# Two-layer mixture of experts behind a channel attention: the gate step of a block of the first layer moves from the steps of the block before it to the block's own

## The chip, the cores and the metric

The kernel runs on one core of a Trainium2 chip. The metric is the time of one execution in microseconds (us) on the device. Engines are named as in the profile: PE is TensorE (PEld its weight loads), DVE is VectorE, ACT is ScalarE, POOL is GpSimd, SP is SyncE. L1891 is line 1891 of the kernel.

## The reference

Three stages run one after the other on 2 x 5056 tokens of 256 channels. The attention's output is the input of the first layer of experts, whose output is the input of the second.

```
# attention over channels (q, k normalised down the tokens)
s = kn.transpose(0, 2, 1) @ qn / tau
a = exp(s - s.max(-1));  a /= a.sum(-1) + 1e-9
x = v @ a                                    # 10112 x 256

# first layer: each token goes to its best of 8 experts
logits = x @ w_gate
e_idx = argmax(logits, axis=1)
gate_w = softmax(logits)[n, e_idx]
eom = 1 / (1 + exp(-(x @ w_output_gate)))
out[mask] = gate_w * eom[:, e] * (relu(x[mask] @ w1[e]) @ w2[e])    # F = 1024

# second layer: experts with a capacity of N // 8, filled in order of the logits
```

The output weight of a first-layer token, gate_w * eom, is one number g for each token. The second layer's gate logits are a product of the first layer's output, so its assignment can only be made when the whole first layer is done.

## The kernel before, in words

The attention is computed first, and each token's row is written to a table in memory (xe_scr). A row holds the 256 channels, the token's gate logits relative to its best one and its output-gate logit (from column ZC on), and a few more numbers (from TC-1 on: the token's number and the like). Rows of one expert are then brought together by indirect transfers.

The first layer works in 33 blocks. A block holds nt = 4, 2 or 1 tiles of 128 tokens, all of one expert. The blocks are taken in the order 4, 4, 1, 2, 4, 2, 4, 1, 2, 4, 4, 1, 2, ... A product in full precision is made of three at lower precision: every operand is split into a high part, which ACT copies, and a low part, which DVE gets by a subtraction (w1h and w1l, w2h and w2l, xh and xl in xhl, hh and hl). One-tile blocks take their first product undivided.

One loop goes over the units of the blocks: 8 of a four-tile block, 4 of the others. In each turn three things are written down, and the framework's scheduler then orders them on each engine, by the buffers that they need and by when it thinks they can run; each engine runs its own queue strictly in that order:

- *ffn1* of the unit: the matmuls pb (L1942), then ACT's hh (L1951) and DVE's hl (L1952).
- *drain* of the unit two turns earlier: the matmuls py (L1970, or L1976 for blocks whose second product is put off until after the second layer's assignment has begun; those need only the gating product py <- hl, gs). Behind a block's last unit stand its output (yout or lout: yo, and l, the second layer's logits, L2004) and order, which makes the key and code rows of the second layer's assignment out of l.
- some *steps* that prepare later blocks, a few per turn from a list that is made at a block's first unit. It has the split steps of block j+1 (s1: w1, L1903 and L1904; sx: transposes of xi, L1882, and xhl, L1884 to L1887; s2: w2, L1908 and L1909; s3: the second layer's gate weights, L1919) and the slot steps of block j+4 (reach: sof and shs, L1672 and L1674; pick: the matmul pt <- tb, shs, L1680; left and count: srl and sju; index: ssi, L1694, which is the list of the rows to fetch). At the same place the weights of block j+2 are loaded (SP, L1814 to L1825), and the rows xi of block j+3 fetched by indirect transfers on POOL, one for each tile (L1697).

The gate step sg is one of the split steps. It takes the logits out of xi into z (L1891, cut at -87), copies the other columns to xk (L1892), and makes g1: an exponential by a polynomial on DVE (the rows gte_t, gte_k, gte_i, L1001 to L1014, with z changed in place), a sum, an add, a product and a reciprocal (L1899). It is 19 DVE rows. yout and lout read xk and g1. z (name z1) has two buffers, xk and g1 three each.

Ahead of the loop stand the split steps of block 0, the fetch of block 1, and the slot steps and fetches of blocks 2 and 3. What stands before that, up to some 208 us, is the end of the attention; the row base (L1558) is one of the last rows of the first layer's assignment.

Of the kernel before, what the change touches and what calls it, by code (L numbers as in the profile page):

```python
# [8 lines left out]
F32 = mybir.dt.float32  # L9
# [13 lines left out]
P = 128  # L23
# [16 lines left out]
AT4, AT1 = (1, 8, 12, 15), (1, 5, 7, 10)  # L40
# [865 lines left out]
def moe_kernel(ctx, tc, q, k, v, tau, wg, wo, w1, w2, wg2, w12, w22, out):  # L906
# [87 lines left out]
    def exp_poly(*args):  # L994
        for _ in exp_steps(*args):
            pass
# [869 lines left out]
    def split_steps(j):  # L1866
# [8 lines left out]
        g1 = pg1.tile([P, nt], F32, name="g1", bufs=3)  # L1875
        xk = pg1.tile([P, nt, XW - TC + 1], F32, name="xk", bufs=3)
        wts[j] = (xk, w1h, w1l, w2h, w2l, xhl, None, g1)
# [10 lines left out]

        def sg(_):
            z = pg1.tile([P, nt, E + 1], F32, name="z1")  # L1890
            V.tensor_scalar(z, xi[:, :, ZC:ZC + E + 1], -87.0, None, op0=ALU.max)  # L1891
            V.tensor_copy(xk, xi[:, :, TC - 1:])  # L1892
            ee = pg1.tile([P, nt, E + 1], F32, name="ee1")
            exp_poly(pg1, ee, z, [P, nt, E + 1], "gte")
            s8 = pg1.tile([P, nt], F32, name="s81")
            V.tensor_reduce(s8, ee[:, :, :E], axis=AX.X, op=ALU.add)
            V.tensor_scalar(s8, s8, 1e-9, None, op0=ALU.add)
            V.scalar_tensor_tensor(s8, ee[:, :, E], 1.0, s8, op0=ALU.add, op1=ALU.mult)
            V.reciprocal(g1, s8)  # L1899
# [21 lines left out]
        steps = [(s1, 0), (sx, 0), (s1, 1), (s1, 2), (sx, 1), (s1, 3), (s2, 0), (s2, 1), (s2, 2), (s2, 3), (sg, 0), (s3, 0)]  # L1921
        return steps if nt > 1 else [x for x in steps if x[0] is not s1]

# [92 lines left out]
    for f_, a_ in [x for i in (0, 2, 3, 5, 1, 4, 6, 7, 8, 9, 10) for x in st_[i:i + 1]] + st_[11:]:  # L2016
        f_(a_)
    ma.close()
    fetch(1)
    for f_, a_ in slot_steps(2):  # L2020
        f_(a_)
    fetch(2)
    for f_, a_ in slot_steps(3):
        f_(a_)
# [21 lines left out]
    for (j, u, n) in units:  # L2046
        if u == 0:
# [3 lines left out]
            if j + 3 < NBLK:  # L2051
                fetch(j + 3)
            if j + 2 < NBLK:
                load(j + 2)
            if j + 4 < NBLK:
                for i, x in zip(AT1 if len(steps) < 12 else AT4, slot_steps(j + 4)):
                    steps.insert(i, x)
            if j in put_off:
                hold(j)
# [3 lines left out]
        for _ in range(SPL[blk(j)[0]]):  # L2063
            if steps:
                f_, a_ = steps.pop(0)
                f_(a_)
    while pend:
        drain()
# [142 lines left out]
```

## Time and profile before

| what | value |
|---|---|
| median of 3 runs | 1385.28 us (1382.11 to 1388.48) |
| the profiled execution, its own time | 1379.16 us |
| its span | 1377.1 us |
| busy, share of the span: PE, PEld | 93%, 84% |
| busy, share of the span: DVE, ACT, POOL | 78%, 58%, 19% |
| granted clock of PE, mean | 0.97 |
| chain that ended last, by engine | PE 43%, DVE 5%, DMA 3%, ACT 1% |

The time is that of the whole execution as the device measures it; the span is from the first to the last instruction that the profiler recorded, so some 2 us lie around it. An engine's busy share counts only its computing instructions. The granted clock is the share of full speed at which TensorE was allowed to run. The chain goes back from the last instruction, at each step to what released it.

### The profile page before, as it was taken

The numbers are of one execution on the slowest core, as the hardware profiler recorded it, in microseconds if no ns is written. First come the engines' busy times: TensorE is split into PE (matmuls) and PEld (weight loads), VectorE is DVE, ScalarE is ACT, GpSimd is POOL, SyncE is SP. The second block draws the span as 40 slices with busy tenths as digits, with TensorE's granted clock in tenths as the row PEclk, the third lists the DMA queues.
The fourth block names the chain that finished last, engine by engine and source line by source line (L and its number), as shares of the span: only waits on it lengthen the run. The fifth ranks groups of instructions, "written<-read, shape, count | busy, mean of one in ns | idle before, by whom it ended". The sixth has DMA issues, their size and how long they took to land.

```text
span 1377.1 us, 25616 instructions
## 1 busy us (share of the span) xinstructions
PE 1281.4 (93%) x8716; PEld 1154.5 (84%) x8716; DVE 1069.5 (78%) x3756; ACT 798.5 (58%) x1752; POOL 267.3 (19%) x367
## 2 busy tenths in 40 slices
PE   8999998999799988999899896989999999999997
PEld 6899866898688977878887896879999999998996
DVE  6887678699588967797688677998999898987321
ACT  5566665466365554574467565766667585755222
POOL 1000012112012021020020002141325051416312
PEclk9999998999899999999999998999999999999999
DMA  8869758196657577095572695030303030314100
GB/s 283 283 218 341 235 164 259 37 296 203 214 163 279 178 249 226 30 340 171 157 242 74 216 409 176 24 116 23 112 29 121 28 119 33 107 63 156 43 24 30
DMA packets 138915, 222.88 MB, mean 162 GB/s; under 512 B 26432, under 2 KB 102336, under 8 KB 136736
## 3 DMA queue, kind: packets, MB, share of 16 engines
q1 hardware_dynamic: 112496, 174.29, 37.5%
q0 software_dynamic: 11808, 32.69, 8.1%
q10 hardware_dynamic: 14480, 14.27, 3.3%
q8 instruction: 69, 1.13, 0.3%
q14 instruction: 62, 0.51, 0.1%
HBM read 170.18 MB, written 50.31 MB: 160 GB/s over the span
## 4 chain that ended last, share of the span: by engine, by line
PE 43%; DVE 5%; DMA 3%; ACT 1%; issue 1%; POOL 1%; DVEq 0%; POOLq 0%; ACTq 0%
PE pb L777 15%; PE py L818 15%; PE pd L2155 4%; PE pb L1942 3%; PE py L1970 2%; DVE junk L377 1%; DMA xi<-xe_scr,ssi 1%; PE pb L739 1%; PE py L816 1%; DMA xi<-y_scr,si 1%; ACT junk L380 1%; PE pb L1937 1%; DVE hl L798 0%; DMA w1r<-in_moe_w_dram 0%; POOL xi L686 0%
## 5 line engine op out<-in xcount | busy, mean ns | idle before, releaser
L1942 PE MATMUL pb<-xhl,w1h 128*128 128x512 f32 (+1 forms) x800 | 217.0, 360 | 2.2 <-ACT xhl L1886 1.6
L1697 POOL DMA_INDIRECT xi<-xe_scr,ssi x86 | 87.3, 1016 | 623.9 <-DVE srl L1685 196.2
L1951 ACT ACTIVATE hh<-pb 128x512 fp32r<-128x512 f32 (+1 forms) x180 | 101.5, 565 | 144.9 <-PE pb L1942 121.5
L818 PE MATMUL py<-w2l,hh 128*128 128x256 f32 (+1 forms) x640 | 182.4, 285 | 0.0
L818 PE MATMUL py<-w2h,hl 128*128 128x256 f32 (+1 forms) x640 | 181.7, 284 | 0.0
L818 PE MATMUL py<-w2h,hh 128*128 128x256 f32 (+1 forms) x600 | 173.2, 289 | 0.0
L790 ACT ACTIVATE hh<-pb 128x512 fp32r<-128x512 f32 (+1 forms) x160 | 93.9, 589 | 132.9 <-PE pb L777 127.0
L798 DVE SCALAR_TENSOR_TENSOR hl<-pb,hh 128x512 fp32r<-128x512 f32 (+1 forms) x160 | 108.4, 678 | 69.2 <-ACT hh L790 69.1
L1942 PEld LDWEIGHTS pb<-xhl,w1h 128*128 128x128 f32 x800 | 137.5, 196 | 19.8 <-ACT xhl L1886 1.8
L1970 PE MATMUL py<-w2h,hh 128*128 128x264 f32 x496 | 147.5, 298 | 6.1 <-DVE l L2004 6.0
L1970 PE MATMUL py<-w2h,hl 128*128 128x264 f32 x496 | 144.7, 292 | 5.1 <-DVE hl L1952 5.1
L1970 PE MATMUL py<-w2l,hh 128*128 128x264 f32 x496 | 145.4, 293 | 0.3 <-DVE w2l L1919 0.3
L1942 PE MATMUL pb<-xhl,w1l 128*128 128x512 f32 (+1 forms) x400 | 140.7, 352 | 0.0
L777 PE MATMUL pb<-xl,w1h 128*128 128x256 f32 (+2 forms) x384 | 139.8, 364 | 0.4 <-DVE xl L747 0.4
L777 PE MATMUL pb<-xh,w1h 128*128 128x256 f32 (+2 forms) x384 | 139.4, 363 | 0.2 <-DVE hl L798 0.2
L777 PE MATMUL pb<-xh,w1l 128*128 128x256 f32 (+2 forms) x384 | 138.9, 362 | 0.0
L844 POOL DMA_INDIRECT out_dram<-yo,ti x80 | 79.4, 993 | 282.0 <-ACT yo L836 242.7
L1952 DVE SCALAR_TENSOR_TENSOR hl<-pb,hh 128x512 fp32r<-128x512 f32 (+1 forms) x180 | 114.4, 637 | 24.1 <-ACT hh L1951 23.2
L818 PEld LDWEIGHTS py<-w2l,hh 128*128 128x128 f32 (+1 forms) x640 | 120.5, 188 | 4.2
L818 PEld LDWEIGHTS py<-w2h,hl 128*128 128x128 f32 (+1 forms) x640 | 120.6, 188 | 1.6
L818 PEld LDWEIGHTS py<-w2h,hh 128*128 128x128 f32 (+1 forms) x600 | 113.0, 188 | 3.8
L1970 PEld LDWEIGHTS py<-w2h,hh 128*128 128x128 f32 x496 | 97.0, 196 | 10.6 <-DVE l L2004 7.4
(530 smaller groups left out, 3444.8 us busy)
## 6 DMA issues: line engine op xcount, KB each, us to landing
w2r<-in_moe_w_dram SPq DMA_DIRECT2D x45, 1024.0 KB, 8.3
w1r<-in_moe_w_dram SPq DMA_DIRECT2D x41, 1024.0 KB, 5.5
vt<-in_v_dram SPq DMA_DIRECT2D x18, 512.0 KB, 7.1
qt<-in_q_dram SPq DMA_DIRECT2D x17, 512.0 KB, 3.7
kt<-in_k_dram SPq DMA_DIRECT2D x17, 512.0 KB, 4.5
xe_scr<-xs ACTq DMA_DIRECT2D x8, 1072.0 KB, 5.8
h_scr<-hh SPq DMA_DIRECT2D x32, 256.0 KB, 3.2
h_scr<-hl SPq DMA_DIRECT2D x32, 256.0 KB, 3.6
```

Of the source, the lines that this page charges most:

```text
L377: V.tensor_scalar(junks[c], x, s.cand[:, c:c + 1], 0.0, op0=ALU.is_ge, op1=ALU.add, accum_out=cnt[:, c:c + 1])
L777: T.matmul(x.pb[:, ci, :n], a[:, c, fc * P:fc * P + P], b_[:, c, xs_], start=(c == 0 and i == 0), stop=(c == 1 and i == 2))
L790: S.activation(x.hh[:, :, :n], x.pb[:, :, :n], AF.Relu)
L798: V.scalar_tensor_tensor(x.hl[f], x.pb[f], 0.0, x.hh[f].bitcast(F32), op0=ALU.max, op1=ALU.subtract)
L818: T.matmul(py[:m_, t % 2, :], a[:, ci, t * P:t * P + m_], b_[:, fc, :], start=False, stop=(fc == 7 and i == 2 and t % 2 == 1))
L844: s_ = G.indirect_dma_start(out=out, out_offset=bass.IndirectOffsetOnAxis(ap=st.ti[:m_, t0 + t:t0 + t + 1], axis=0), in_=q.yo[:m_, t % 2, ...
L1697: nc.gpsimd.indirect_dma_start(out=xi[:, i, :], out_offset=None, in_=xe, in_offset=bass.IndirectOffsetOnAxis(ap=self.si[:, i:i + 1], axis=0))
L1942: T.matmul(o, a[:, c, ws], xhl[:, c, h, :], start=(i == 0), stop=(i == 5))
L1951: S.activation(hh, pb, AF.Relu)
L1952: V.scalar_tensor_tensor(hl, pb, 0.0, hh.bitcast(F32), op0=ALU.max, op1=ALU.subtract)
L1970: T.matmul(py[t][:, :width], a[:, ci, ts_], b_[:, fc, :width], start=(fc == 0 and i == 0), stop=(fc == 7 and i == 2))
L2155: T.matmul(py[t][:, :D], a[:, ts_], b_[:, fc, :D], start=(fc == 0 and i == 0), stop=(fc == 7 and i == 2))
```

## The change

The gate step is no longer one of the split steps of the block ahead. It is a function gate_step(j) and stands among the steps that are worked off during block j itself, at place 6 of the list. z and xk become two parts of one buffer, zk, of which there is one: the next block's zk can only be written when yout or lout of the last block has read it. g1 has two buffers in place of three. The slot steps and fetches of blocks 2 and 3 move from the stretch ahead of the loop into the list of block 0, together with those of block 4 (at places 2, 9 and 15; block 0 takes four steps per unit). The places of the slot steps in the other lists shift by one, since the list is one shorter ahead of them. All lists must now be done by their block's last unit.

```
--- before.py
+++ after.py
@@ -37,7 +37,8 @@
 NCH = {4: 1, 2: 2, 1: 2}
 HS, XS, FS = 1, 1, 3
 PLAG, PHB = 2, 4
-AT4, AT1 = (1, 8, 12, 15), (1, 5, 7, 10)
+AT4, AT1 = (1, 8, 11, 14), (1, 5, 7, 9)
+GAT = {4: 6, 2: 6, 1: 6}
 KS1, KS2 = 16, 28
 KST = (KS1, KS2)
 KO4, KO2, KO1 = 0.0, 0.97, 0.5
@@ -1872,9 +1873,7 @@
         w2l = pws.tile([P, 8, D + E], F32R, name="w2l")
         xhl = pxi.tile([P, 2, 2, nt * P], F32R, name="xhl")
         xh, xl = xhl[:, :, 0, :], xhl[:, :, 1, :]
-        g1 = pg1.tile([P, nt], F32, name="g1", bufs=3)
-        xk = pg1.tile([P, nt, XW - TC + 1], F32, name="xk", bufs=3)
-        wts[j] = (xk, w1h, w1l, w2h, w2l, xhl, None, g1)
+        wts[j] = [xi, w1h, w1l, w2h, w2l, xhl, None, None]
 
         def sx(c):
             pt = qt_.tile([P, 512], F32, name="pt")
@@ -1886,18 +1885,6 @@
             S.copy(xh[:, c, :], pt[:, :nt * P])
             V.tensor_tensor(xl[:, c, :], pt[:, :nt * P], xh[:, c, :].bitcast(F32), op=ALU.subtract)
 
-        def sg(_):
-            z = pg1.tile([P, nt, E + 1], F32, name="z1")
-            V.tensor_scalar(z, xi[:, :, ZC:ZC + E + 1], -87.0, None, op0=ALU.max)
-            V.tensor_copy(xk, xi[:, :, TC - 1:])
-            ee = pg1.tile([P, nt, E + 1], F32, name="ee1")
-            exp_poly(pg1, ee, z, [P, nt, E + 1], "gte")
-            s8 = pg1.tile([P, nt], F32, name="s81")
-            V.tensor_reduce(s8, ee[:, :, :E], axis=AX.X, op=ALU.add)
-            V.tensor_scalar(s8, s8, 1e-9, None, op0=ALU.add)
-            V.scalar_tensor_tensor(s8, ee[:, :, E], 1.0, s8, op0=ALU.add, op1=ALU.mult)
-            V.reciprocal(g1, s8)
-
         def s1(i):
             c, f = i // 2, slice(i % 2 * 512, i % 2 * 512 + 512)
             S.copy(w1h[:, c, f], w1r[:, c, f])
@@ -1918,8 +1905,25 @@
                 S.copy(w2h[:, :, D:], wgr)
                 V.tensor_tensor(w2l[:, :, D:], wgr, w2h[:, :, D:].bitcast(F32), op=ALU.subtract)
 
-        steps = [(s1, 0), (sx, 0), (s1, 1), (s1, 2), (sx, 1), (s1, 3), (s2, 0), (s2, 1), (s2, 2), (s2, 3), (sg, 0), (s3, 0)]
+        steps = [(s1, 0), (sx, 0), (s1, 1), (s1, 2), (sx, 1), (s1, 3), (s2, 0), (s2, 1), (s2, 2), (s2, 3), (s3, 0)]
         return steps if nt > 1 else [x for x in steps if x[0] is not s1]
+
+    def gate_step(j):
+
+        nt, xi = blk(j)[0], wts[j][0]
+        zk = pg1.tile([P, nt, E + 1 + XW - TC + 1], F32, name="zk", bufs=1)
+        g1 = pg1.tile([P, nt], F32, name="g1")
+        wts[j][0], wts[j][7] = zk[:, :, E + 1:], g1
+        z = zk[:, :, :E + 1]
+        V.tensor_scalar(z, xi[:, :, ZC:ZC + E + 1], -87.0, None, op0=ALU.max)
+        V.tensor_copy(zk[:, :, E + 1:], xi[:, :, TC - 1:])
+        ee = pg1.tile([P, nt, E + 1], F32, name="ee1")
+        exp_poly(pg1, ee, z, [P, nt, E + 1], "gte")
+        s8 = pg1.tile([P, nt], F32, name="s81")
+        V.tensor_reduce(s8, ee[:, :, :E], axis=AX.X, op=ALU.add)
+        V.tensor_scalar(s8, s8, 1e-9, None, op0=ALU.add)
+        V.scalar_tensor_tensor(s8, ee[:, :, E], 1.0, s8, op0=ALU.add, op1=ALU.mult)
+        V.reciprocal(g1, s8)
 
     def ffn1(j, u, w, nt):
 
@@ -2013,15 +2017,10 @@
     for j in (4, 5):
         sls[j].table()
     st_ = split_steps(0)
-    for f_, a_ in [x for i in (0, 2, 3, 5, 1, 4, 6, 7, 8, 9, 10) for x in st_[i:i + 1]] + st_[11:]:
+    for f_, a_ in [x for i in (0, 2, 3, 5, 1, 4, 6, 7, 8, 9) for x in st_[i:i + 1]] + st_[10:]:
         f_(a_)
     ma.close()
     fetch(1)
-    for f_, a_ in slot_steps(2):
-        f_(a_)
-    fetch(2)
-    for f_, a_ in slot_steps(3):
-        f_(a_)
     units = []
     for j in range(NBLK):
         nt = blk(j)[0]
@@ -2048,22 +2047,29 @@
             steps = split_steps(j + 1) if j + 1 < NBLK else []
             if j + 6 < NBLK:
                 sls[j + 6].table()
-            if j + 3 < NBLK:
+            if 0 < j and j + 3 < NBLK:
                 fetch(j + 3)
             if j + 2 < NBLK:
                 load(j + 2)
-            if j + 4 < NBLK:
-                for i, x in zip(AT1 if len(steps) < 12 else AT4, slot_steps(j + 4)):
+            if not j:
+                for k, i in ((2, 2), (3, 9), (4, 15)):
+                    for x in slot_steps(k) + ([(lambda _, k=k: fetch(k), 0)] if k < 4 else []):
+                        steps.insert(i, x)
+                        i += 1
+            elif j + 4 < NBLK:
+                for i, x in zip(AT1 if len(steps) < 11 else AT4, slot_steps(j + 4)):
                     steps.insert(i, x)
+            steps.insert(GAT[blk(j)[0]], (lambda _, j=j: gate_step(j), 0))
             if j in put_off:
                 hold(j)
         pend.append((j, u, n, ffn1(j, u, wts[j], blk(j)[0])))
         if len(pend) > PLAG:
             drain()
-        for _ in range(SPL[blk(j)[0]]):
+        for _ in range(SPL[blk(j)[0]] if j else 4):
             if steps:
                 f_, a_ = steps.pop(0)
                 f_(a_)
+        assert u < n - 1 or not steps
     while pend:
         drain()
     mp.close()
```

What it does to the order of the instructions, on DVE. The lines of the changed kernel are shifted: z is L1918, xk L1919, hl L1956, l L2008, w2l L1896, w1l L1891, the gate rows L1002 to L1015. A number behind a name tells tiles of the same name apart; x2 means twice in a row.

The first place is the end of block 8 (two tiles) and the two four-tile blocks behind it, 9 and 10. Before, z_5264 belongs to block 9 and z_5565 to block 10, and yo to block 8; the ssi at the top is the list of rows for a later fetch:

```order
L1694 SCALAR_TENSOR_TENSOR ssi<-ssl,pt 128x4
L1952 SCALAR_TENSOR_TENSOR hl<-pb,hh 128x512
L1909 TENSOR_TENSOR w2l<-w2r,w2h 128x2x256 x2
L1952 SCALAR_TENSOR_TENSOR hl<-pb,hh 128x512
L1909 TENSOR_TENSOR w2l<-w2r,w2h 128x2x256
L1892 COPY xk<-xi 128x8
L1899 RECIPROCAL g_4879<-s_5051 128x2
L1919 TENSOR_TENSOR w2l<-wgr,w2h 128x8x8
L1891 TENSOR_SCALAR z_5264<-xi 128x36
L1952 SCALAR_TENSOR_TENSOR hl<-pb,hh 128x512
L1001 TENSOR_SCALAR gte_t<-z_5264 128x36
L2001 COPY yo<-xk 128x2x4
```

The row behind these is the next z:

```order
L1891 TENSOR_SCALAR z_5565<-xi 128x36
L1003 TENSOR_SCALAR gte_k<-gte_t 128x36
L1001 TENSOR_SCALAR gte_t<-z_5565 128x36
L1004 SCALAR_TENSOR_TENSOR z_5264<-gte_k,z_5264 128x36
L1013 TENSOR_SCALAR gte_i<-gte_k 128x36
```

After, at the l rows of block 8 (l_2781 <- py, g_5148) and behind them; the zk row is that of block 9:

```order
L2008 TENSOR_SCALAR l_2781<-py,g_5148,zk 128x8
L1891 TENSOR_TENSOR w1l<-w1r,w1h 128x512
L2008 TENSOR_SCALAR l_2781<-py,g_5148,zk 128x8
L1886 TENSOR_TENSOR xhl<-pt,xhl 128x512
L1791 TENSOR_SCALAR key_t<-l_2781 128x16
L1802 TENSOR_TENSOR ord_g<-l_2781 128x128
L1792 TENSOR_TENSOR key_t<-l_2781,key_t 128x16
L1956 SCALAR_TENSOR_TENSOR hl<-pb,hh 128x512
L1795 COPY key<-key_t 128x8x2 x2
L1803 TENSOR_TENSOR ord_g<-ord_g,tri_226 128x128
L1918 TENSOR_SCALAR zk<-xi 128x4x9
L1919 COPY zk<-xi 128x4x4
```

Before, the z of both blocks stands ahead of the l rows of block 8, with one hl, one gte_t and yo between them. After, zk of block 9 stands behind the l rows of block 8; that of block 10 follows 53 rows later, behind the l rows of block 9.

The second place is a two-tile block, 12, from the key row of the block before it (11, one tile) on. Before:

```order
L1794 COPY key<-key_t 128x8 x2
L1802 TENSOR_TENSOR ord_g<-ord_g,tri_226 128x64
L1904 TENSOR_TENSOR w1l<-w1r,w1h 128x512
L1805 TENSOR_REDUCE ord_a<-ord_g 128x8
L1806 TENSOR_REDUCE ord_b<-ord_g 128x8
L1909 TENSOR_TENSOR w2l<-w2r,w2h 128x2x256
L1807 TENSOR_TENSOR ord_a<-ord_a,ord_b 128x8
L1952 SCALAR_TENSOR_TENSOR hl<-pb,hh 128x512
L1808 SCALAR_TENSOR_TENSOR code<-ord_a,c_228 128x8
L1909 TENSOR_TENSOR w2l<-w2r,w2h 128x2x256 x3
L1952 SCALAR_TENSOR_TENSOR hl<-pb,hh 128x512
L1685 SCALAR_TENSOR_TENSOR srl<-rh,k2o,pt 128x1
```

After:

```order
L1795 COPY key<-key_t 128x8 x2
L1803 TENSOR_TENSOR ord_g<-ord_g,tri_226 128x64
L1918 TENSOR_SCALAR zk<-xi 128x2x9
L1919 COPY zk<-xi 128x2x4
L1806 TENSOR_REDUCE ord_a<-ord_g 128x8
L1807 TENSOR_REDUCE ord_b<-ord_g 128x8
L1002 TENSOR_SCALAR gte_t<-zk 128x18
L1891 TENSOR_TENSOR w1l<-w1r,w1h 128x512
L1808 TENSOR_TENSOR ord_a<-ord_a,ord_b 128x8
L1004 TENSOR_SCALAR gte_k<-gte_t 128x18
L1956 SCALAR_TENSOR_TENSOR hl<-pb,hh 128x512
L1809 SCALAR_TENSOR_TENSOR code<-ord_a,c_228 128x8
```

Before, there is no gate row in this block (they stand in a four-tile block ahead of it); after, the block's own gate rows stand between its w2l, hl and w1l rows and the key and code rows of the block before.

The third place is the start of the experts' part. Before, around the row base_333 of the first layer's assignment:

```order
L1558 TENSOR_TENSOR ones__332<-left,k1n 128x8
L1558 SCALAR_TENSOR_TENSOR ones__332<-ones__332,odd 128x8
L1558 SCALAR_TENSOR_TENSOR base_333<-k1n,base 128x8
L1558 TENSOR_TENSOR tmp_279<-lt,ones__332 128x64
L1558 TENSOR_REDUCE kc_298<-tmp_279 128x8
L1558 TENSOR_SCALAR kc_298<-kc_298 128x8
L1468 TENSOR_TENSOR wl<-pt,wh 128x512
```

After:

```order
L1559 TENSOR_TENSOR ones__332<-left,k1n 128x8
L1559 SCALAR_TENSOR_TENSOR ones__332<-ones__332,odd 128x8
L1559 SCALAR_TENSOR_TENSOR base_333<-k1n,base 128x8
L1918 TENSOR_SCALAR zk<-xi 128x4x9
L1559 TENSOR_TENSOR tmp_279<-lt,ones__332 128x64
L1919 COPY zk<-xi 128x4x4
L1002 TENSOR_SCALAR gte_t<-zk 128x36
L1559 TENSOR_REDUCE kc_298<-tmp_279 128x8
L1004 TENSOR_SCALAR gte_k<-gte_t 128x36
```

After, the zk of block 0 is moved up to right behind base_333, and the following gate rows stand between the rows of the assignment and wl, the last split weights of the attention. The queues of SP and POOL have the same order before and after.

## Rows read from the trace of the kernel before

**Rows 1.** Busy time by stretches: length, busy time per engine, granted clock, DMA share, GB/s.
```profile
210.50:762.50 552.00, 504.77 (x3306) 447.56 (x3306) 437.43 (x1699) 306.43 (x750) 80.75 (x82) 0.95 0.60 194
340.00:380.00 40.00, 30.07 (x188) 27.08 (x187) 24.39 (x105) 14.57 (x33) 5.12 (x5) 0.83 0.69 227
497.00:530.00 33.00, 23.32 (x158) 21.95 (x157) 20.12 (x92) 12.38 (x28) 0.94 (x1) 0.84 0.61 189
645.00:715.00 70.00, 61.49 (x469) 58.76 (x468) 51.71 (x209) 38.72 (x102) 12.52 (x12) 0.96 0.59 190
```

**Rows 2.** VectorE's waits, 210 to 765: total, times, longest.
```profile
DVE z L1891 <- DMA xi<-xe_scr,ssi: 59.4, 16, 7.3
...
DVE z L1891 <- issue: 2.7, 1, 2.7
```

**Rows 3.** TensorE's waits, 210 to 765.
```profile
PE py L1976 <- DVE hl L1952: 13.0, 6, 4.7
...
PE pt L1680 <- DVE xhl L1887: 11.1, 3, 5.3
...
PE py L1970 <- DVE l L2004: 6.0, 3, 2.6
...
PE py L1970 <- DVE hl L1952: 5.1, 1, 5.1
...
PE pt L1882 <- issue: 2.4, 1, 2.4
...
PE py L1975 <- DVE l L2004: 2.0, 1, 2.0
...
PE pt L1680 <- DVE shs L1674: 1.6, 1, 1.6
```

**Rows 4.** Timeline of one stall: start, duration, engine, operation, idle before.
```profile
344.45 0.95 POOL L1697 DMA_INDIRECT xi<-xe_scr,ssi  x1 [0.30 <-issue]
...
350.50 0.18 DVE L1891 TENSOR_SCALAR z<-xi 128x36 f32<-128x36 f32 x1 [6.34 <-DMA xi<-xe_scr,ssi]
...
352.31 0.60 PE L1976 MATMUL py<-hl,gs 128*8 128x512 f32 x1 [4.67 <-DVE hl L1952]
```

**Rows 5.** Timeline of TensorE at two later gaps.
```profile
615.04 0.40 PE L1976 MATMUL py<-hl,gs 128*8 128x512 f32 x1 [1.78 <-DVE hl L1952]
...
691.42 0.31 PE L1680 MATMUL pt<-tb,shs 128*128 128x82 bf16 x4 [0.59 <-DVE xhl L1887]
```

**Rows 6.** Timeline of VectorE: rows of gate steps.
```profile
351.20 0.17 DVE L1014 TENSOR_SCALAR gte_i<-gte_i 128x36 int32<-128x36 int32 x1
...
351.29 0.19 DVE L1004 SCALAR_TENSOR_TENSOR z<-gte_k,z 128x36 f32<-128x36 f32 x1
...
408.24 1.12 DVE L1009 SCALAR_TENSOR_TENSOR gte_t<-gte_t,z 128x36 f32<-128x36 f32 x5
```

**Rows 7.** Busy time between the l rows of one block and the next.
```profile
320.95:333.69 12.74, 12.61 (x94) 11.71 (x93) 12.40 (x37) 9.47 (x26) 2.21 (x3) 1.00 0.80 256
592.49:602.82 10.33, 10.22 (x74) 9.60 (x74) 10.27 (x31) 8.28 (x20) 3.37 (x4) 1.00 1.08 355
356.06:383.59 27.53, 22.27 (x155) 21.56 (x154) 18.20 (x61) 13.68 (x33) 2.35 (x3) 0.86 0.74 245
507.26:533.93 26.67, 21.42 (x153) 20.74 (x152) 18.11 (x61) 13.65 (x32) 2.34 (x3) 0.87 0.76 220
```

**Rows 8.** Timeline at the start of the experts' part.
```profile
205.47 0.16 DVE L1558 SCALAR_TENSOR_TENSOR base<-k1n,base 128x8 f32<-128x8 f32 x1
...
205.66 0.97 POOL L1697 DMA_INDIRECT xi<-xe_scr,ssi  x1 [0.30 <-issue]
...
208.34 0.66 PE L1882 MATMUL pt<-ident,xi 128*128 128x128 f32 x4
```

**Rows 9.** Timeline of SyncE: one weight load.
```profile
358.18 0.41 SPq L1814 DMA_DIRECT2D w1r<-in_moe_w_dram  x1
```

**Rows 10.** ScalarE's waits for weights, 210 to 765.
```profile
ACT w1h L1903 <- DMA w1r<-in_moe_w_dram: 4.2, 4, 1.8
```

## The prediction

> **What bounds the kernel now.** I read the table of engines first: TensorE (PE) is busy 93% of the span, so time can only come from its idle stretches and from stretches at the lower clock. Then the busy time by stretches: the experts' part of the first layer, 210.5 to 762.5 us, is 552.0 us in which PE is busy 504.8 and idle 47.2, with a mean granted clock of 0.95 [rows 1]. So even here some 90% of the time is matmul work, and a change to small VectorE (DVE) rows can matter only through that idle time and the clock.
>
> Third, the waits. The reader is to see that one DVE row stands out: z, the first row of a gate step, waits 59.4 us in 16 cases for the transfer of xi (its tokens' rows), and 2.7 us once more with no releaser shown [rows 2]. Nothing else on DVE waits like that for memory. The waits of PE show who pays: it waits for DVE's hl, xhl and l, which need no memory at all [rows 3]. The timeline of one case joins the two: the last fetch of xi for a four-tile block starts on GpSimd at 344.45; DVE stands from about 344 to 350.50 at the z that reads it; PE, whose next matmul reads an hl that is queued behind that z, stands for 4.67 us until 352.31 [rows 4]. DVE issues in order, so rows that could run are held by one that can't.
>
> **The change, term by term.** The edits: the gate step of block j leaves the end of block j-1's steps and stands among j's own; z and xk share one buffer zk, where z had two and xk three; the slot steps and fetches of blocks 2 and 3 leave the stretch ahead of the loop for block 0. The order of instructions shows what the scheduler made of it: before, the z of block 10 stands right behind z and hl of a block before it, a few rows behind the row that gives the fetch its indices; after, zk of a block always stands behind the l rows of the block ahead, and by then its matmuls have been running on xi for a while. The new wait (zk must be read by the output of the last block) costs nothing: yo, l and xm, which read it, are DVE rows that stand ahead of it in the same queue.
>
> *Term 1, idle PE that comes back.* Six rows of PE's waits end on DVE rows or on a transpose behind one: 13.0, 11.1, 6.0, 5.1, 2.4 and 2.0 us [rows 3]. I followed the gaps over 0.3 us in them; all but two come within some 8 us behind a z wait. These two, 1.78 us at 615.04 and 0.59 us at 691.42 [rows 5], come where DVE was simply busy. So 39.6 - 2.4 = 37.2 us.
>
> *Term 2, the clock.* In the stretches with the long gaps the granted clock falls to its lower level of 1.2 GHz for a while: the means are 0.83 in 340 to 380, 0.84 in 497 to 530 and 0.96 in 645 to 715 [rows 1]. Work done there at half speed costs busy time times (1 - clock): 30.07 x 0.17 + 23.32 x 0.16 + 61.49 x 0.04 = 5.1 + 3.7 + 2.5 = 11.3 us. If the gaps go, I take that this goes too.
> The Trainium skill ("TensorE: Matmul & The Clock Gate", section "Terms") puts the penalty at the throttled time times (1 - K/N), that is without weighting by the busy share. By that formula the same three stretches would give 6.8 + 5.3 + 2.8 = 14.9 us, and the sum below would be 3.6 us lower. PE was idle in part of those stretches, and that idle time is in term 1 already, so the rows speak for the smaller number.
>
> *Term 3, what DVE can't deliver.* A gate step is 19 DVE rows. Interleaved with others, such rows start 0.09 us apart; alone, each waiting for the one before, 0.22 us apart (five in 1.12 us) [rows 6]. That bounds its price: 1.7 to 4.2 us. In the order after the change most gate rows have a w1l, w2l, hl or key row between them, so I take 1.7.
> Before, all gate rows lie in the four-tile blocks (some of them three steps together), where DVE has time; none in most of the one- and two-tile blocks. After, every block has its own. From the l rows of one block to those of the next, DVE is busy 12.40 of 12.74 us and 10.27 of 10.33 us in two of the short blocks, while PE too is busy nearly throughout [rows 7]. There are eight such among the nineteen short blocks, with 0.06 to 0.92 us free on DVE and 4.0 us in sum. Eight gates of 1.7 us less 4.0 us free are 9.6 us that PE will wait.
> In the two stretches with the worst stalls the gain is also capped by DVE. From 356.06 to 383.59 PE needs 22.27 x 0.86 = 19.2 us at full clock; DVE needs 18.20 plus two gates, 21.6, and at the best rate shown (12.40 of 12.74, 0.97) 22.3 us: 3.1 us do not come back. From 507.26 to 533.93 it is 21.42 x 0.87 = 18.6 against (18.11 + 3.4)/0.97 = 22.2: 3.6 us [rows 7]. Together 6.7 us.
>
> *Term 4, the start.* The zk of block 0 is now placed right behind the row base at 205.47, while the last fetch of block 0's rows is only issued at 205.66; the transposes that read them start at 208.34 [rows 8]. So DVE will stand there some 3.0 us, with the wl, w1l and xhl rows behind it on which ACT and PE wait next, and the first matmul of the experts comes that much later. Against it, the gap of 1.6 us behind shs [rows 3] should go, since the gate and the sof rows of two slots no longer stand between the w2l and the hl of block 0. Net 1.4 us lost; bounds 0 (if xi lands as early as 206.6, its issue's end) and 4.
>
> Slots 2 to 4 of block 0 and the fetches behind them come later than before, but rows for block 2 are first transposed in block 1, some 20 us on; SP's and GpSimd's rows keep their order, so no queue is passed. I cost this at nothing; it would show as a wait of PE's transposes for xi.
>
> **Sum:** -37.2 - 11.3 + 9.6 + 6.7 + 1.4 = -30.8 us. The profiled execution took 1379.2 us, so 1348.4 us on its own scale. It lay 6.1 us under the median of the three timed runs, 1385.3 us; on the scale of the median the forecast is 1354.5 us. About 0.5%, 7 us, is what a measurement of this kernel can tell from no change (the three runs spread over 6.4 us).
>
> **Rivals.**
> *All of it comes back* (terms 1 and 2 in full, DVE never the last): -48.5 us, 1337 us. For it: rows of DVE that nobody needs at once (order's key and code rows) can fall behind for a while without harm. Against it: DVE's queue is in order, and in the short blocks it is already full [rows 7].
> *Weight loads take the place of the stalls.* w1r for the block after next can be loaded only when a one-tile block's matmuls have read the buffer: issued at 358.18 [rows 9], and ACT waits for w1r 4.2 us in four cases today, 1.8 at most [rows 10]. If PE no longer pauses, that wait may appear behind each of the eight one-tile blocks: 8 x 1.8 = 14.4 us, 1369 us. Against it: the loads start earlier too, since what releases them runs earlier.
> *The change doesn't do what it says*: some other DVE row that waits for memory (sof for its table, w1l for w1r) stands in front of hl as z did, and the stalls stay. With the 1.4 us of the start, 1387 us. Against it: DVE's waits show no such row above 0.5 us, and they stand where they did.
> *Slower: the gate's chain is the bound of the short blocks.* If its 19 rows run one by one there, 4.2 instead of 1.7 us: 2.5 us more in the eight full blocks (20.0), four times in the two capped stretches (10.3 at 0.97), and about 6 in three more that have only 1.7 to 2.8 us free. That is 36 us, all the gain and 5 more: 1391 us. It decides from some 3.8 us per short block on. For it: in a one-tile block of the new order four gte_t rows do stand in a row, and g must be ready ahead of yo and l.
> A rule of the Trainium skill speaks for this one: "VectorE: DVE Perf Modes", section "The TRN2 errata — SBUF-src ops pay a fixed extra latency per instruction", gives a small DVE operation a measured fixed term of about 150 cycles at 0.96 GHz whatever its size. As an estimate from that page a gate row of 36 elements is (36 + 150)/0.96 = 194 ns and a step 3.7 us, which would put the kernel at about 1384 us. The rows agree on how long one row takes, but show that the next one starts after 0.09 us where it does not depend on it [rows 6], so I give it little.
>
> **How the numbers follow.** Forecast (1354.5) 0.64; all comes back 0.12; weight loads 0.12; no effect 0.06; gate chain 0.06. The range reaches from a little under the second case to beyond the third: 1333 to 1376 us, some 0.83 of the whole. The first three cases are faster by over 0.5%; I leave 0.01 of them for a sum off by more than that: faster 0.87. No effect and part of the gate chain give within 0.5%: 0.07; slower by over 0.5%: 0.06.
>
> **What would show it.** Right: no wait of zk for xi but the one at the start (about 3 us there); PE's waits for hl at the gating matmuls and for xhl at the slot matmuls near zero; the experts' part about 521 us long instead of 552.0, with the clock near 1.00 where it was 0.83; DVE busy 0.95 or more in the short blocks, with gate rows in them, and PE waiting there for l or xhl by a microsecond or two. Wrong: w1h waiting for w1r in most one-tile blocks; other DVE rows waiting for memory; or the l rows of the short blocks 2 us and more later than now, block after block. A gain in the second layer's part, which the change doesn't touch, would also say that I read it wrongly.

## The result and the profile after

The changed kernel takes 1339.01 us in the median of four runs (1336.04 to 1340.76), the kernel before 1383.99 us beside it. The ratio is 0.9668, with a 95% interval of 0.9638 to 0.9699: faster by 45 us. The forecast was 1354.5 us with a range of 1333 to 1376, so the time lies inside, 15.5 us below the forecast and 2 us from the rival in which all of it comes back (1337).

The profiled execution took 1340.76 us with a span of 1339.0, so the spans differ by 38.1 us. To see where, I cut the experts' part at two DVE rows that both kernels have, the row base of the first layer's assignment and the last l row; what follows is the second layer. First the busy time by stretches of the kernel before (columns as in rows 1):

```profile
205.47:763.45 557.98, 508.20 (x3331) 449.69 (x3332) 442.61 (x1720) 309.87 (x757) 84.67 (x85) 0.95 0.60 193
763.45:1377.10 613.65, 580.08 (x4127) 534.93 (x4125) 470.77 (x1578) 358.74 (x736) 174.70 (x260) 0.98 0.30 103
```

The same view of the changed kernel: the experts' part, the second layer, one stretch that answers to the first stall of before, then four stretches between l rows that answer to [rows 7]:

```profile
206.41:715.93 509.52, 492.81 (x3331) 437.00 (x3331) 430.88 (x1720) 308.64 (x757) 87.25 (x85) 0.98 0.65 211
715.93:1339.00 623.07, 584.73 (x4127) 539.10 (x4125) 471.00 (x1578) 358.84 (x736) 175.90 (x260) 0.97 0.30 101
340.00:380.00 40.00, 39.59 (x284) 36.08 (x283) 37.95 (x162) 24.53 (x60) 5.08 (x5) 1.00 0.80 275
318.11:331.25 13.14, 12.83 (x98) 12.12 (x97) 12.71 (x52) 9.70 (x28) 2.37 (x3) 1.00 0.60 181
559.10:571.76 12.66, 12.66 (x84) 11.28 (x84) 12.21 (x51) 9.55 (x22) 3.06 (x3) 1.00 1.07 362
347.42:368.29 20.87, 20.46 (x157) 19.36 (x156) 19.76 (x90) 14.01 (x34) 2.49 (x3) 1.00 0.87 298
481.24:502.02 20.78, 20.29 (x155) 19.18 (x154) 19.77 (x90) 13.88 (x33) 2.52 (x3) 1.00 0.86 238
```

The reader is to see three things. The experts' part, on the same 3331 matmuls, is 48.5 us shorter: PE's idle time in it goes from 49.8 to 16.7 us (33.1 less), its busy time from 508.2 to 492.8 us (15.4 less), and the clock from 0.95 to 0.98. In 340 to 380, where PE was busy 30.07 us at a clock of 0.83 [rows 1], it is busy 39.59 at 1.00. And the second layer, which the change doesn't touch, was 9.4 us longer in this execution; the last experiment comes back to that.

DVE's waits in the experts' part of the changed kernel:

```profile
DVE hl L1956 <- ACT hh L1955: 39.2, 34, 3.1
...
DVE zk L1918 <- DMA xi<-xe_scr,ssi: 3.1, 1, 3.1
```

The 59.4 us in 16 cases of [rows 2] are one case of 3.1 us, that of the start. PE's waits there:

```profile
PE pn L1477 <- DVE wl L1469: 3.7, 1, 3.7
PE pt L1681 <- DVE xhl L1886: 3.0, 6, 1.0
PE pb L1946 <- DVE hl L1956: 1.9, 1, 1.9
PE pt L1881 <- issue: 1.5, 1, 1.5
PE py L1980 <- DVE hl L1956: 0.9, 1, 0.9
```

Of the two largest of [rows 3], the wait for hl at the gating matmuls falls from 13.0 to 0.9 us, that for xhl at the slot matmuls from 11.1 to 3.0. New is the wait for wl at the start. Its timeline:

```profile
206.41 0.16 DVE L1559 SCALAR_TENSOR_TENSOR base<-k1n,base 128x8 f32<-128x8 f32 x1
209.67 0.38 DVE L1918 TENSOR_SCALAR zk<-xi 128x36 f32<-128x36 f32 x1 [3.10 <-DMA xi<-xe_scr,ssi]
210.50 0.68 DVE L1469 TENSOR_TENSOR wl<-pt,wh 128x512 fp32r<-128x512 f32 x1
211.24 0.59 PE L1477 MATMUL pn<-wl,gh 128*8 128x512 f32 x1 [3.75 <-DVE wl L1469]
```

DVE stands 3.10 us at the zk of block 0, as the order of instructions foretold, the wl row stands behind it, and PE waits for that.

### The profile page after: what moved, and what is told of

Same layout as the page of the kernel before. It is cut to its first block, busy times and chain, and to the rows that moved or that the text cites. A ratio compares the mean times of both kernels' runs of the same rounds, so it can differ in the third digit from the quotient of the medians.

```text
span 1339.0 us, 25615 instructions
## 1 busy us (share of the span) xinstructions
PE 1270.5 (95%) x8716; PEld 1145.4 (86%) x8716; DVE 1058.2 (79%) x3756; ACT 797.5 (60%) x1752; POOL 271.1 (20%) x367
## 4 chain that ended last, share of the span: by engine, by line
PE 76%; DVE 8%; DMA 8%; ACT 4%; issue 2%; POOL 1%; SPq 1%; DVEq 0%; ACTq 0%; POOLq 0%
PE pb L778 16%; PE py L819 16%; PE pb L1946 13%; PE py L1974 10%; PE pd L2161 4%; PE ps L1105 3%; PE px L1337 3%; DMA w1r<-in_moe_w_dram 3%; DMA kt<-in_k_dram 2%; PE px L1341 1%; DVE junk L378 1%; DMA xi<-y_scr,si 1%; PE pb L740 1%; PE pb L1941 1%; PE pt L1316 1%
## 5 line engine op out<-in xcount | busy, mean ns | idle before, releaser
L1946 PE MATMUL pb<-xhl,w1h 128*128 128x512 f32 (+1 forms) x800 | 214.2, 356 | 3.3 <-DVE hl L1956 1.9
L1956 DVE SCALAR_TENSOR_TENSOR hl<-pb,hh 128x512 fp32r<-128x512 f32 (+1 forms) x180 | 114.7, 637 | 40.9 <-ACT hh L1955 39.2
L1974 PE MATMUL py<-w2h,hh 128*128 128x264 f32 x496 | 143.7, 291 | 0.5 <-DVE l L2008 0.5
L1974 PE MATMUL py<-w2l,hh 128*128 128x264 f32 x496 | 141.1, 285 | 0.9 <-DVE w2l L1906 0.9
L1974 PE MATMUL py<-w2h,hl 128*128 128x264 f32 x496 | 141.3, 285 | 0.0
L687 POOL DMA_INDIRECT xi<-y_scr,si x80 | 82.2, 1027 | 82.1 <-issue 27.9
```

The source lines that it names most:

```text
L687: G.indirect_dma_start(out=st.xi[:n, r, :], out_offset=None, in_=ys, in_offset=bass.IndirectOffsetOnAxis(ap=st.si[:n, r:r + 1], axis=0))
L1946: T.matmul(o, a[:, c, ws], xhl[:, c, h, :], start=(i == 0), stop=(i == 5))
L1956: V.scalar_tensor_tensor(hl, pb, 0.0, hh.bitcast(F32), op0=ALU.max, op1=ALU.subtract)
L1974: T.matmul(py[t][:, :width], a[:, ci, ts_], b_[:, fc, :width], start=(fc == 0 and i == 0), stop=(fc == 7 and i == 2))
```

## The experiments

Twelve kernels (after_again is the changed one once more), timed in three groups, each against the kernel before beside it. The kernel before took 1423.6, 1432.6 and 1426.8 us in these groups, some 40 us more than in the runs above. The profiles put that into the second layer (see after_again), so the absolute whole times in the expectations don't hold for any of them; ratios and the length of the experts' part do. The part is cut as above: 557.98 us before, 509.52 us after.

| kernel | ratio to before, 95% | experts' part, us |
|---|---|---|
| own_apart | 1.0008 (0.9981 to 1.0034) | 555.75 |
| start_only | 1.0025 (1.0002 to 1.0048) | 560.02 |
| old_zk3 | 0.9661 (0.9614 to 0.9707) | 504.36 |
| own_zk2 | 0.9641 (0.9601 to 0.9682) | 504.85 |
| gate_only | 0.9656 (0.9581 to 0.9730) | 509.51 |
| gate0_late | 0.9651 (0.9564 to 0.9738) | 512.74 |
| gate_none | 0.9679 (0.9605 to 0.9752) | 509.41 |
| short_twice | 0.9828 (0.9755 to 0.9901) | 532.60 |
| short_extra | 0.9626 (0.9595 to 0.9658) | 508.81 |
| old_zk2 | 0.9646 (0.9617 to 0.9675) | 506.80 |
| zk2_late_start | 0.9621 (0.9595 to 0.9648) | 504.92 |
| after_again | 0.9640 (0.9615 to 0.9664) | 510.25 |

### Place or buffer: own_apart, old_zk3, own_zk2, start_only

The change has a new place, a joined buffer, one buffer in place of several, and a new start. The four runs take them apart.

**own_apart**: the new place, z and xk apart.

```
-        zk = pg1.tile([P, nt, E + 1 + XW - TC + 1], F32, name="zk", bufs=1)
+        xk = pg1.tile([P, nt, XW - TC + 1], F32, name="xk", bufs=1)
+        z = pg1.tile([P, nt, E + 1], F32, name="z1")
```

> The changed kernel, but z and xk are two buffers again (z two of them, xk one); the gate step keeps its new place. The order of instructions puts every z back where it stood before, up to three blocks ahead. Theory A (the gain comes from z being tied to the buffer that the last outputs read, which keeps it from running ahead to a transfer that has just been issued): the waits of z for xi are back, 55 to 60 us in about 15 cases, and the time is within 8 us of the kernel before, 1376 to 1392 us. Theory B (the gain comes from the new place among the block's own steps): within 8 us of the changed kernel, 1331 to 1347 us.

**old_zk3**: the old place, z and xk joined (against before; **old_zk2**, below, is the same with bufs=2).

```
-        xk = pg1.tile([P, nt, XW - TC + 1], F32, name="xk", bufs=3)
+        zk = pg1.tile([P, nt, E + 1 + XW - TC + 1], F32, name="zk", bufs=3)
+        z, xk = zk[:, :, :E + 1], zk[:, :, E + 1:]
...
-            z = pg1.tile([P, nt, E + 1], F32, name="z1")
```

> The kernel before, with one edit: z and xk are parts of one buffer of which there are three; the gate step keeps its old place in the steps of the block before. The order of instructions puts z of block j behind the l rows of block j-3 at the earliest. Theory A: that is far enough behind the fetch; no z waits for xi by more than 1 us behind the start, and the time is 1332 to 1352 us. Theory B: the place is the old one, so the time is that of before, 1376 to 1392 us.

**own_zk2**: the changed kernel with `bufs=2` for zk.

> The changed kernel with two buffers zk in place of one; z of block j then stands behind the l rows of block j-2. Theory A: no z waits for xi, as in the changed kernel; 1331 to 1347 us. Theory C (it takes the one buffer: with two the z rows run ahead again and meet their transfers): some 20 to 30 us of z waits, 1350 to 1370 us.

**start_only**: the kernel before with the start of the changed one.

```
     fetch(1)
-    for f_, a_ in slot_steps(2):
-        f_(a_)
-    fetch(2)
-    for f_, a_ in slot_steps(3):
-        f_(a_)
...
+            if not j:
+                for k, i in ((2, 2), (3, 9), (4, 15)):
+                    for x in slot_steps(k) + ([(lambda _, k=k: fetch(k), 0)] if k < 4 else []):
+                        steps.insert(i, x)
+                        i += 1
```

> The kernel before with only the slot steps and fetches of blocks 2 and 3 moved into block 0. Theory A: the start is worth 0 to 3 us: 1378 to 1388 us, with z's waits for xi at 55 to 60 us. Theory D (a good part of the gain is the start, where slots and fetches stood ahead of the first block's weights): 1365 to 1375 us.

DVE's waits and the experts' part of own_apart:

```profile
DVE z L1918 <- DMA xi<-xe_scr,ssi: 68.3, 19, 7.6
```

```profile
205.05:760.80 555.75, 504.95 (x3331) 448.05 (x3331) 440.01 (x1721) 310.42 (x757) 84.17 (x85) 0.95 0.59 193
```

The experts' part of old_zk3 (no z there waits for xi at all), and of own_zk2:

```profile
206.01:710.37 504.36, 489.38 (x3331) 435.17 (x3331) 438.62 (x1720) 309.95 (x757) 87.61 (x85) 0.99 0.66 213
```

```profile
206.98:711.83 504.85, 490.74 (x3331) 436.41 (x3332) 437.21 (x1720) 309.07 (x757) 88.49 (x85) 0.98 0.65 213
```

That settles the main question. With the new place but z on its own buffers, the waits are back (68.3 us in 19 cases) and nothing is gained. With the old place but z joined to xk, they are gone and all is gained. So Theory A stands and B and C fall: what counts is that z shares a buffer that the outputs of an earlier block must have read. That keeps the scheduler from placing z right behind the row that starts its transfer, and one, two or three such buffers are all far enough, behind the start (own_zk2 has two waits, 3.1 and 2.4 us, of blocks 0 and 1). The place in the block's own steps gains nothing by itself, and start_only, at 560.0 us and with 63.1 us of z waits, shows no gain from the start. Not tried is a z of its own with one buffer, which would tell how late a release must be.

### What VectorE's rows cost: gate_none, short_twice, short_extra

The prediction charged 16.3 us for DVE rows that PE would wait for. gate_none leaves the arithmetic out; its output weight is a constant, so its second layer has other numbers to sort and only its experts' part is compared:

```
-        V.tensor_scalar(z, xi[:, :, ZC:ZC + E + 1], -87.0, None, op0=ALU.max)
...
-        V.reciprocal(g1, s8)
+        V.tensor_scalar(g1, xi[:, :, ZC + E], 0.0, 0.5, op0=ALU.mult, op1=ALU.add)
```

> The changed kernel without the gate step's arithmetic (17 of its 19 VectorE rows are left out in every block, the output weight is the constant 0.5). Theory P: VectorE is still last in the short blocks and gets 33 x 1.7 us of time back; the experts' part becomes 8 to 14 us shorter, 495 to 502 us. Theory Q: the gate rows cost TensorE almost nothing any more; 0 to 4 us shorter, 505 to 510 us (the wait at the start stays, since the copy of xi stands where zk stood).

short_twice puts the whole arithmetic into a loop:

```
+        for _ in range(2 if nt < 4 and j < 24 else 1):
+            V.tensor_scalar(z, xi[:, :, ZC:ZC + E + 1], -87.0, None, op0=ALU.max)
...
+            V.reciprocal(g1, s8)
```

> The changed kernel with the gate step's arithmetic done twice in the thirteen one- and two-tile blocks ahead of block 24 (18 more VectorE rows in each; the second pass repeats the first). The length of the experts' part, from the row base to the last l row, is 509.5 us in the changed kernel. Theory P (as predicted: what VectorE can't deliver in a short block, TensorE waits for there): 13 x 1.7 us less the 7.8 us that VectorE has free in these blocks, so some 14 us more, 521 to 527 us. Theory Q (the rows of a full short block are finished in the four-tile block behind it, where VectorE has time, while TensorE runs on): at most 4 us more, 508 to 514 us.

short_extra has as many rows more, on other tiles:

```
         V.reciprocal(g1, s8)
+        if nt < 4 and j < 24:
+            z2 = pg1.tile([P, nt, E + 1], F32, name="z2")
+            V.tensor_scalar(z2, ee, -1.0, None, op0=ALU.mult)
+            e2 = pg1.tile([P, nt, E + 1], F32, name="ee2")
+            exp_poly(pg1, e2, z2, [P, nt, E + 1], "gtf")
...
```

> The changed kernel with the same 18 more VectorE rows in the same thirteen short blocks as in the run that does the gate step twice, but on buffers of their own, behind the exponential of the gate and with a result that nothing reads. Theory R (there the l rows came 4 to 8 us late because the output weight was only ready after two gate chains one behind the other): the experts' part is at most 8 us longer than 509.5, 508 to 518 us. Theory S (it was the number of VectorE rows): as there, 525 to 535 us.

The experts' part of the three, in this order:

```profile
210.58:719.99 509.41, 489.78 (x3331) 436.23 (x3331) 381.64 (x1159) 309.45 (x757) 84.94 (x85) 0.98 0.65 211
```

```profile
204.84:737.44 532.60, 498.18 (x3331) 441.49 (x3331) 457.42 (x1955) 308.90 (x757) 87.86 (x85) 0.97 0.62 202
```

```profile
208.23:717.04 508.81, 491.73 (x3331) 435.80 (x3331) 447.05 (x1954) 308.08 (x757) 91.06 (x85) 0.99 0.65 211
```

With 234 rows more that no output waits for, the part does not grow. The same number costs 23.1 us where the output weight is at their end, more than both theories had said. With 561 rows fewer (1159 against 1720) the part as a whole is no shorter, but that length hides two things. Cut at the first l row of block 0, gate_none has

```profile
210.58:257.53 46.95, 36.15 (x192) 29.30 (x192) 26.02 (x78) 21.00 (x53) 12.40 (x12) 0.82 0.64 201
257.53:719.99 462.46, 453.63 (x3141) 406.93 (x3140) 355.62 (x1082) 288.45 (x706) 72.54 (x73) 1.00 0.65 212
```

and the changed kernel, in its two profiles (after, after_again),

```profile
206.41:249.82 43.41, 35.38 (x192) 28.96 (x192) 27.24 (x95) 21.11 (x53) 12.54 (x12) 0.84 0.70 218
249.82:715.93 466.11, 457.43 (x3141) 408.04 (x3140) 403.64 (x1627) 287.52 (x706) 74.71 (x73) 1.00 0.64 210
```

```profile
205.34:246.56 41.22, 33.22 (x192) 27.35 (x193) 27.12 (x94) 21.15 (x53) 12.55 (x12) 0.92 0.72 229
246.56:715.59 469.03, 458.81 (x3141) 409.49 (x3140) 403.94 (x1628) 287.77 (x706) 75.91 (x73) 0.99 0.64 209
```

At the start gate_none has a stall of its own making: the row that writes g of block 1 reads the fresh xi and waits 2.49 us for it, and PE waits 2.1 us behind that. Behind block 0 it is 3.7 and 6.6 us shorter than the two. So the gate rows do have a price there, some 4 to 7 us of the 16.3, with the reserve that the two profiles of the same program differ by 2.9 us. That is short of Theory P's 8 to 14 us. And what short_twice pays for is not how many rows DVE has (S falls), but when g is ready (R). PE's largest wait in short_twice is this:

```profile
PE py L1975 <- DVE l L2009: 9.2, 4, 4.0
```

and the l row of block 2, the first block with a doubled step, in short_twice, in short_extra and in the changed kernel stands at

```profile
291.27 0.29 DVE L2009 TENSOR_SCALAR l<-py,g,zk 128x8 f32<-128x8 f32 x1 [0.52 <-ACT yo L2008]
```

```profile
286.15 0.28 DVE L2018 TENSOR_SCALAR l<-py,g,zk 128x8 f32<-128x8 f32 x1
```

```profile
283.65 0.29 DVE L2008 TENSOR_SCALAR l<-py,g,zk 128x8 f32<-128x8 f32 x1
```

From each kernel's base row (204.84, 208.23, 206.41) that is 86.4, 77.9 and 77.2 us: 9 us late with two chains in a row, 0.7 us with the same rows off the chain. The last row of the chain, which makes g, stands in short_twice and in the changed kernel at

```profile
289.80 0.16 DVE L1927 RECIPROCAL g<-s 128x1 f32<-128x1 f32 x1
```

```profile
282.84 0.15 DVE L1926 RECIPROCAL g<-s 128x1 f32<-128x1 f32 x1
```

that is 85.0 and 76.4 us from the base row: g is 8.5 us late and the l row with it. A late l holds the accumulators py of its block, and PE's next products need them. One doubt remains: in short_twice the next block's single zk is freed late as well, which is part of the same delay and was not separated from it.

### The start: gate_only, gate0_late, zk2_late_start, old_zk2

gate_only is the changed kernel with the start of before. gate0_late is the changed kernel and one row more:

```
         z = zk[:, :, :E + 1]
+        if not j:
+            V.tensor_scalar(zk[:, 0, :], wts[0][2][:, 1, F - (E + 1 + XW - TC + 1):].bitcast(F32), 0.0, None, op0=ALU.mult)
```

zk2_late_start joins both, with two buffers zk.

> The changed kernel with the slot steps and fetches of blocks 2 and 3 ahead of the loop, as before. If the start change is worth nothing or a little loss, as its run alone says (560.0 against 558.0 us), the experts' part is 506 to 511 us; if the later slots of block 0 are a gain that only shows without the z waits, 512 to 516 us.

> The changed kernel with one more small VectorE row that writes zk of block 0 from the last columns of its w1l, so that the gate step of block 0 can't stand ahead of w1l. If the wait of 3.1 us at the start and the 3.75 us for which TensorE then waits for wl are on the path, the experts' part is 3 to 4 us shorter, 505 to 507 us. If the transposes wait for xi there anyhow, it is within 1 us, 508 to 511 us.

> The changed kernel with two buffers zk, the start of before, and block 0's gate step held behind its w1l by one small row. If ScalarE's wait of 3.2 us at the start of the run with that row alone was a matter of that execution, the experts' part is 500 to 504 us; if it comes again, 503 to 508 us.

> The kernel before with one edit: z and xk are parts of one buffer of which there are two; the gate step keeps its old place, and the start is as before. If the changed kernel's loss against this kind (some 4 us behind block 0 through a gate step that ends late in the short blocks, some 3 us at the start) is a matter of the single buffer and of the place of block 0's gate, this is the shortest experts' part of all: the start of the run with three buffers (40 us to the l row of block 0) and from there that of the run with two (461.5 us), 500 to 504 us. If the place in the block's own steps is a gain of its own, it is 506 us or more.

The start of before gives 509.51 us, the same as the changed one. gate0_late took 512.74 us, above both of its ranges. The wait for wl is gone, but ScalarE's first xhl copy comes late, in its timeline:

```profile
213.58 0.58 ACT L1885 CAST xhl<-pt 128x512 fp32r<-128x512 f32 x1 [3.20 <-remote]
```

The profile names nothing on this core that ends these 3.20 us, so its cause stays open. In zk2_late_start it doesn't come; there the zk of block 1 now stands between the added row and the zk of block 0, and waits for its own transfer:

```profile
216.52 0.18 DVE L1920 TENSOR_SCALAR zk<-xi 128x36 f32<-128x36 f32 x1 [4.79 <-DMA xi<-xe_scr,ssi]
```

Its part, 504.92 us, missed the 500 to 504 us and is that of own_zk2 (504.85), which still has the wait for wl. So I found no version in which taking the stall at the start out of the changed kernel shortens the part. What the stall costs stays open: old_zk3 and old_zk2, where no z waits there, reach the l row of block 0 in 40.25 and 40.91 us, the changed kernel in 43.41 and 41.22, with a granted clock of 0.84 and 0.92 in that stretch.

The five profiles with one buffer and no more work on the chain lie at 508.8 to 510.3 us (gate0_late apart), the four with two or three at 504.4 to 506.8. The cause of these 2 to 6 us is not shown. A g that is ready late in short blocks fits in part. With one zk a gate step can only begin when the block before has put out its rows, and in the 19 short blocks of the changed kernel g is ready only 0.5 to 2.4 us ahead of the first l row; in gate_none it is 11.8 us or more, in own_zk2 between 0.6 and 23.0. And gate_none, behind block 0, is as short (462.46 us) as the four (461.48 to 465.89). Against it stands old_zk2, where g is ready 7.5 us ahead or more and the stretch behind block 0 still takes 465.89 us, as long as in one profile of the changed kernel; 2 to 3 us are also what a piece of the part varies by in the same program. old_zk2 was to be the shortest of all and is not (506.80): its start is as short as was said (40.91 us), the rest is not (461.5 was expected). By its own expectation that speaks for a gain of 2 us from the new place; old_zk3, in the old place and the shortest of all, speaks against it. As whole times the best, zk2_late_start, has 0.9621 (0.9595 to 0.9648) against 0.9640 (0.9615 to 0.9664) of the changed kernel beside it; that is not told apart.

### The second layer: after_again

> The changed kernel once more, beside the others on this chip. The experts' part repeats to 1 us: 508.5 to 510.5 us. What differs in the second layer (623 us in the first profile of the changed kernel, 614 us before) is then a matter of the chip and the execution, not of the change: it should be within 10 us of the second layer in the other kernels' profiles here.

The experts' part repeats as a whole (510.25 against 509.52 us); its two pieces, above, differ by 2.2 and 2.9 us in opposite directions. The second layer of after_again, and that of start_only, whose experts' order is that of before:

```profile
715.59:1370.20 654.61, 596.16 (x4127) 545.02 (x4125) 471.89 (x1578) 358.65 (x736) 174.21 (x260) 0.96 0.28 96
```

```profile
766.21:1426.20 659.99, 596.23 (x4127) 546.18 (x4125) 471.62 (x1578) 358.63 (x736) 173.47 (x260) 0.95 0.28 95
```

It takes 654.6 and 660.0 us in these runs with either order, 613.7 and 623.1 us in the first two profiles. In the twelve kernels it lies between 653.99 and 667.56 us, and not by which order the experts have. So the 9.4 us by which it was longer in the first profile of the changed kernel are not shown to be the change's. The three groups ran on three chips, and no run here separates the chip from the execution.

## Why the prediction was right, and where it was off

**The bound and the stall.** Right. The time came from PE's idle stretches and the lower clock in the experts' part, and the cause was the z row that stood ahead of its transfer in DVE's queue. own_apart and old_zk3 show this from both sides: the waits go with z's buffer, and the time goes with the waits. I had read the change as a move behind the l rows of the block ahead; that the new place has no part in it I had not seen. The order had shown the right consequence all the same.

**Term 1, 37.2 us of idle time.** PE's idle time in the experts' part fell by 33.1 us, with the new 3.75 us at the start in it, so by 36.8 us without. The term was right.

**Term 2, 11.3 us from the clock.** PE's busy time fell by 15.4 us on the same matmuls. The term counted three stretches; [rows 1] gives 0.95 for the whole part, so the clock was low outside of them too. A little too small. The Trainium skill's formula ("TensorE: Matmul & The Clock Gate", section "Terms"), without the busy share, had given 14.9 us for the three stretches. Over the whole part the traces' clock records decide: TensorE stood at its lower level for 51.2 us before and 17.1 after, and was busy in 44.4 and 13.7 us of these. Half of the difference is 17.1 us without the busy share and 15.3 with it; 15.4 were measured.

**Term 3, 16.3 us that VectorE can't deliver.** This is the step that failed, and it accounts for most of the difference from the forecast. It charged each full short block 1.7 us for its gate rows, at once and to PE. The short blocks did become as full as said: DVE is busy 12.71 of 13.14 us and 12.21 of 12.66 in two of them, and their l rows lie 0.4 and 2.3 us further apart than before. But PE is idle only 0.31 and 0.00 us there: it runs on into the next block. In the two stretches that I took as capped, DVE needed 19.76 and 19.77 us, not the 21.6 and 21.5 of the sum, and they took 20.87 and 20.78 us, not 22.3 and 22.2. short_extra shows 234 such rows more as costing nothing where nobody waits for them. gate_none shows what is left of the term: some 4 to 7 us of the 16.3; whether that is paid where DVE is full or where an l row waits for a late g is open.

**Term 4, 1.4 us at the start.** The 3.10 us at zk and PE's 3.75 us behind it came as predicted, but the start change by itself is worth nothing (gate_only), and taking the stall away brought nothing (zk2_late_start). The wait was right; its price is not shown.

**The rivals.** *All of it comes back* is where the time landed, and its reason is right in kind: short_extra shows that rows which nobody needs at once cost nothing. But its example isn't: in the changed kernel the code rows end no later behind the l rows than before (a median of 3.4 us against 3.8). Which rows fall behind instead was not followed. I had given it 0.12 because I held a full queue for a late one. *Weight loads*: w1h waits for w1r 5.1 us in four cases, 2.3 at most, against 4.2 us [rows 10]; it did not come up behind each one-tile block. *No effect*: no other row waits for memory as z did. *The gate's chain*: it does not take all the gain, but the mechanism is real. In the changed kernel g is ready just ahead of the l rows, and the 4 to 7 us of gate_none are the most that can be put down to it; made twice as long in thirteen short blocks, the chain costs 23.1/13 = 1.8 us in each.
What the Trainium skill says of small rows ("VectorE: DVE Perf Modes", section "The TRN2 errata — SBUF-src ops pay a fixed extra latency per instruction") agrees with the length of the rows here, 0.14 to 0.19 us for a small one, but the forecast of some 1384 us worked out from it is refuted by the 1339: rows of other work stand between dependent ones (in the timeline of block 2 in the changed kernel, an hl, w1l or xhl row between most of the last rows of the gate step).

## What to carry to other kernels

In a queue that runs strictly in order, look first for rows that wait for memory, and for who stands behind them; sixteen small rows of some 0.18 us each were worth 48 us here. Where a scheduler places rows by the buffers that they need, a row that reads a fresh transfer can be held back by giving it a buffer whose release comes late enough, and the number of buffers decides how far ahead it may run; the place in the source may decide nothing. And an engine that is busy all through a stretch is not yet the bound: ask for the row that somebody waits for, and when it is done, before charging its neighbours' rows to the sum.

## What was unexpected of the hardware

The distance from one block's l rows to the next repeats to some 0.05 us between executions and groups of runs in many blocks: block 1 takes 21.90 us in the changed kernel, in gate_only, in gate0_late and in after_again. It doesn't in all: block 15 takes 16.40 us in one profile of the changed kernel and 17.96 in the other, and the 192 matmuls up to the l row of block 0 took PE 35.38 us at a granted clock of 0.84 and 33.22 at 0.92. The second layer of the same instructions took 613.7 to 667.6 us over all profiles, with PE idle for 33.6 us in the first and 68.7 us in the longest.
